# Q, K, V, the gate matrices and the noise laid out by numpy in kernel(), with no transposes of Q and K on the chip

## The chip, the core and the metric

The kernel runs on one core of a Trainium2 chip. The metric is the device time of one execution in microseconds. The core's engines are TensorE (PE, with PEld for its weight loads), VectorE (DVE), ScalarE (ACT), GpSimd (POOL) and SyncE (SP, which here only issues DMAs). What numpy does in `kernel()` before the launch is not part of the metric.

## The reference

Three layers follow each other. Attention comes first: 4 batches, 8 heads, 768 positions, 64 columns per head; each chunk of 32 queries sees 8 memory keys, 16 positions to its left, itself and 8 positions to its right. The result, as 3072 tokens of 512 columns, goes through a soft mixture of 8 experts with 4 slots each, and that through a routed mixture of 8 experts in which every token takes its two best after noise.

```python
k_full = np.concatenate([mem_k, k_ctx], axis=2)      # per chunk of 32 queries
v_full = np.concatenate([mem_v, v_ctx], axis=2)
scores = scale * np.matmul(q_c, k_full.transpose(0, 1, 3, 2))
...                                                  # softmax
out[:, :, c_start:c_end] = np.matmul(a, v_full)
# soft layer: logits = x @ phi; slots = softmax(logits, 0).T @ x; relu(slots @ w1) @ w2; softmax(logits, 1) @ that
# routed layer: logits = x @ w_gate + log1p(exp(x @ w_noise)) * noise; top 2; sum of p * relu(x @ w1) @ w2
```

## The kernel before

**Units and blocks.** Attention runs over 16 units (a batch and a pair of heads), each in two halves of 12 chunks; a half is a block here, 32 in all, `i` in the code. One iteration of the main loop issues for every engine, in a fixed order: the scores of block i+1 (`qk`), their maximum, difference and exponential (`mxr`, `sub`, `expo`), the transpose of the exponentials of block i (`at`, copied by `atc`), the product with V of block i-1 (`av`, divided by `nrm`), and the transpose of the result of block i-2 (`xt`, copied by `xtc`). In every second block the soft layer's logits of a group are multiplied or turned (`lg`, `lt`). Iterations 0 to 27 are this loop; the last four blocks, mixed with the soft layer's first sums, stand in the hand-written list `ORDER`. Each engine takes its instructions strictly in that order.

**Q and K.** `load_raw` brings raw Q or K of a unit as it lies in HBM; `tr` turns it with six fp32 transposes on PE into PSUM, and four copies on ACT put it into `QT` or, with room for the memory keys, into `KB`. `fill_mem` copies the 8 memory keys between the chunks of `KB`, on POOL. `KB` is a block of 128 partitions by two halves: head h lives on partitions 64h to 64h+63 and in half h, and the other half there is zero, so that one matmul computes both heads. There are two `KB`, two `QT` and three raw buffers.

**V.** `load_v` brings V of a block, for each head onto 32 partitions, in rows of 256 B (64 columns of one position). Rows 32 to 55 of a head are the same V one chunk further on, which `shift` copies on the chip (head 0 on DVE, head 1 on POOL); rows 56 to 63 are the memory values, which `mem_rows` copies on POOL. A column of ones gives the sum. There are four such buffers, and `load_v(i + 3)` is issued behind `av(i - 1)`.

**DMA.** All these loads are issued by SP in program order, together with pieces of the soft layer's weights (`load_piece`, 512 KB each, 16 during attention, 48 behind it) and of the output's zeroing (`zero_piece`, by the table `ZA`, 384 KB a step). `KB`, the raw buffers and `VB` lie in a part of `big` that the weights take over when attention is done; so do the outputs `xs` when their sums are done. Behind the 48 pieces SP issues the 8 pieces of the first routed expert (`first_load`). While these flow, the soft layer's experts run on PE; the routed layer starts when its first expert has landed, and takes some 320 us.

**Gates and noise.** Between attention and the soft experts POOL issues five loads: constants, two gate matrices, fp16 constants, and the noise.

Of the kernel before, what the change touches and what calls it, by code (L numbers as in the profile page):

```python
# [14 lines left out]
OP = mybir.AluOpType  # L15
# [15 lines left out]
VC = 130  # L31
# [10 lines left out]
ZA = {2: (0, 1), 13: (1, 2), 17: (2, 3), 21: (3, 4), 25: (4, 5), 26: (5, 7), 27: (7, 8)}  # L42
RA, RB = 26, 44
ORDER = [('qk', 29), ('mx', 29), ('tr', 31), ('sub', 29), ('exp', 29), ('av', 27), ('mv', 29), ('sp', 28), ('nrm', 27), ('lt', 5), ('ltc', 5), ('qk', 30), ('max', 0), ('at', 28), ('atc', 28), ('mx', 30), ('qk', 31), ('col', 0), ('at', 29), ('sub', 30), ('atc', 29), ('pc', 15), ('exp', 30), ('colc', 0), ('av', 28), ('mv', 30), ('sp', 29), ('bc', 0), ('nrm', 28), ('pc', 14), ('xt', 26), ('dsub', 0), ('mx', 31), ('xtc', 26), ('ex', 0), ('sub', 31), ('ldv', 31), ('exp', 31), ('at', 30), ('atc', 30), ('av', 29), ('sp', 30), ('mv', 31), ('sp', 31), ('xt', 28), ('xt', 27), ('mm', 0, 0, 0), ('nrm', 29), ('at', 31), ('atc', 31), ('xtc', 27), ('xtc', 28), ('av', 30), ('nrm', 30), ('xt', 29), ('av', 31), ('xt', 30), ('mm', 0, 0, 1), ('xtc', 29), ('xtc', 30), ('lg', 6), ('nrm', 31), ('mm', 0, 1, 1), ('xt', 31), ('lgc', 6), ('xtc', 31), ('es', 0), ('lg', 7), ('lt', 6), ('lgc', 7), ('lt', 7), ('ltc', 6), ('esp', 0), ('mm', 0, 2, 1), ('ltc', 7), ('mm', 0, 3, 1), ('mm', 0, 1, 0), ('max', 1), ('col', 1), ('mm', 0, 2, 0), ('colc', 1), ('bc', 1), ('dsub', 1), ('fac',), ('mm', 0, 3, 0), ('ex', 1), ('mm', 1, 0, 0), ('facx',), ('out', 0, 0), ('out', 0, 1), ('es', 1), ('mm', 1, 1, 0), ('esp', 1), ('out', 1, 0), ('w',), ('mm', 1, 0, 1), ('mm', 1, 1, 1), ('sit', 0), ('out', 1, 1), ('sitc', 0), ('sit', 1), ('sitc', 1)]
# [82 lines left out]
def tile_kernel(ctx, tc, q, k, v, mem_k, mem_v, phi, sw1, sw2, wg, wn, noise, mw1, mw2, cf_in, c16_in, out):  # L127
# [16 lines left out]
    with ExitStack() as sctx:  # L144
# [28 lines left out]
        with ExitStack() as actx:  # L173
            ab = actx.enter_context(tc.tile_pool(name="ab", bufs=1))
            wk = actx.enter_context(tc.tile_pool(name="wk", bufs=2))
            ps = actx.enter_context(tc.tile_pool(name="ps", bufs=1, space=PSUM))

            attention(tc, nc, q, k, v, mem_k, mem_v, phi, xs, L, K, phis, arena, ab, wk, ps, load_piece, zero_piece)
# [888 lines left out]
def attention(tc, nc, q, k, v, mem_k, mem_v, phi, xs, L, K, phis, arena, ab, wk, ps, load_piece, zero_piece):  # L1067
# [17 lines left out]
    mkT = carve(HP * B * NMEM).rearrange("p (c b m) -> p c b m", c=HP, b=B)  # L1085
    XT = [wk.tile([128, 4, 384], F32, name=f"xT{z}", bufs=1) for z in range(2)]
    mkr = XT[0].rearrange("p j n -> p (j n)")[:H * NMEM, :B * 2 * D].rearrange("p (b z d) -> p b z d", b=B, z=2)
# [6 lines left out]
    QT, ST, A, AT, AV = {}, {}, {}, {}, {}  # L1094

    def load_raw(n):
        u, x = divmod(n, 2)
        b, hp = divmod(u, HP)
        src = (q, k)[x]
        o = src.offset + (b * H + 2 * hp) * S * D  # L1100
        w, r = ((768, 1), (256, 3))[x]
        nc.sync.dma_start(RW[n % 3].rearrange("p (t e) -> p t e", t=r),
                          bass.AP(tensor=src.tensor, offset=o, ap=[[w, 128], [128 * w, r], [1, w]]))

    def vcols(i, p, n, col, cols, c0=0, c1=NH):
        return custom(VB[i % NV][p:p + n], c0 * VC + col, [[VC, c1 - c0], [1, cols]])

    def load_v(i):
        u, z = divmod(i, 2)
        b, hp = divmod(u, HP)  # L1110
        for h in range(2):
            o = v.offset + (b * H + 2 * hp + h) * S * D + NH * z * 32 * D
            c0 = 1 if i == 0 and h == 0 else 0
            c1 = NH if i == 2 * NU - 1 and h == 1 else NH + 1

            def piece(row, n, a, e):
                nc.sync.dma_start(vcols(i, 64 * h + row, n, 66 * h, D, a, e),
                                  bass.AP(tensor=v.tensor, offset=o + (row - 16) * D + a * 32 * D,
                                          ap=[[D, n], [32 * D, e - a], [1, D]]))

            if c0:
                piece(16, 16, 0, 1)
            piece(0, 32, c0, c1)
            if c1 == NH:
                piece(0, 16, NH, NH + 1)

    def mem_rows(i):
        for h in range(2):
            p = 64 * h + 32
            nc.gpsimd.tensor_copy(vcols(i, p, 32, 66 * h, D),  # L1130
                                  mvs[p:p + 32, i // 2:i // 2 + 1, :].to_broadcast([32, NH, D]))
# [5 lines left out]
    def fill_mem(u, eng=nc.gpsimd):  # L1137
        b, hp = divmod(u, HP)
        for h in range(2):
            p = 64 * h  # L1140
            o = custom(KB[u % 2][p:p + 64, h, 32:], 0, [[40, NCH], [1, NMEM]])
            eng.tensor_copy(o, mkT[p:p + 64, hp, b:b + 1, :].to_broadcast([64, NCH, NMEM]))

    def tr(n):
        u, x = divmod(n, 2)
        if x == 0:
            QT[u] = wk.tile([128, S], F32, name="qT")
        p = ps.tile([128, 1024], F32, name="tr", bufs=1)
# [15 lines left out]
        if n + 3 < 2 * NU:  # L1164
            load_raw(n + 3)
# [328 lines left out]
```

## Time and profile before

| | us |
|---|---|
| median of 3 runs (lowest to highest) | 531.72 (531.41 to 531.77) |
| profiled execution, its own time | 533.19 |
| its span in the trace | 531.40 |

The span is what the trace shows between the first and the last instruction; the times of the rows count from its start. A row of the windows gives the stretch, its length, the busy time of PE, PEld, DVE, ACT and POOL with the number of instructions in brackets, the granted clock of PE (1.00 is 2.4 GHz), the busy share of the 16 DMA engines (it can exceed 1, since packets overlap) and the GB/s moved. A row of the timeline or the chain begins with the start and the duration; "x24" is the number of instructions merged in it, and "<-" in brackets names what ended an engine's idle time. In groups by form the two numbers behind the bar are the busy time and the mean duration of one in ns. One qk of a block counts 24 matmuls in the trace, since an fp32 matmul runs as two.

### The profile page before, as it was taken

How to read it: one execution, taken by the hardware profiler on the slowest of the kernel's cores; microseconds unless marked ns; L12 is line 12 of the kernel's file. 1: busy time of each engine (PE TensorE's matmuls, PEld its weight loads, DVE VectorE, ACT ScalarE, POOL GpSimd, SP SyncE). 2: the span in 40 equal slices, each digit the busy share in tenths (PEclk: the TensorE clock that was granted, in tenths of full speed). 3: DMA queues.
4: the chain of work that ended last, by engine and by line, in shares of the span. 5: the costliest groups of instructions: out<-in, count | busy, mean ns of one | idle time of the engine just before them, and what ended most of it. 6: DMA issues, size and time to landing. Idle time of an engine off the chain costs nothing.

```text
span 531.4 us, 12425 instructions
## 1 busy us (share of the span) xinstructions
PE 488.7 (92%) x4854; PEld 271.2 (51%) x4854; DVE 323.9 (61%) x748; ACT 258.7 (49%) x456; POOL 260.2 (49%) x320
## 2 busy tenths in 40 slices
PE   3899998988878888999999999999999999999994
PEld 2666666766433425455454445454544544455441
DVE  6599999989852006896658665674584575552310
ACT  4788887877210206364438254273272462543221
POOL 5877887777030000553735355355336563454223
PEclk9899999999998999999999999999999999999998
DMA  9699999999999999795884939647667773353345
GB/s 201 180 243 237 239 271 241 247 231 316 407 408 358 412 410 344 228 315 169 187 257 107 285 56 222 185 98 189 178 158 166 160 202 48 43 66 44 44 56 64
DMA packets 86178, 109.89 MB, mean 207 GB/s; under 512 B 39408, under 2 KB 52656, under 8 KB 86112
## 3 DMA queue, kind: packets, MB, share of 16 engines
q1 hardware_dynamic: 76240, 93.52, 58.5%
q0 software_dynamic: 9456, 15.36, 20.3%
q8 instruction: 40, 0.66, 0.5%
q14 instruction: 26, 0.21, 0.1%
q10 hardware_dynamic: 416, 0.15, 0.1%
HBM read 88.36 MB, written 20.64 MB: 205 GB/s over the span
## 4 chain that ended last, share of the span: by engine, by line
PE 70%; DMA 14%; ACT 6%; POOL 4%; issue 3%; DVE 2%; POOLq 0%; SPq 0%; DVEq 0%; ACTq 0%
PE l L777 44%; DMA big<-in_v_dram 5%; PE l L747 4%; DMA big<-in_moe_w_dram 3%; PE tr L1153 3%; PE st L1177 3%; PE g L383 2%; ACT big L1163 2%; PE av L1223 2%; PE l L774 2%; PE po L272 2%; DMA w<-in_moe_w_dram 2%; ACT qT L1163 2%; PE p L258 2%; DMA cg<-table,idx 1%
## 5 line engine op out<-in xcount | busy, mean ns | idle before, releaser
L777 PE MATMUL l<-big,hi 128*128 128x512 f16 x768 | 174.2, 379 | 0.2 <-ACT hi L751 0.2
L802 POOL DMA_INDIRECT out_dram<-y,C x46 | 77.5, 1685 | 125.9 <-ACT ctt L709 75.7
L759 DVE SCALAR_TENSOR_TENSOR lo<-l,hi 128x1024 f16<-128x1024 f32 x50 | 61.1, 1222 | 101.5 <-ACT hi L751 101.5
L777 PEld LDWEIGHTS <-hi 128*128 128x128 f16 x768 | 72.6, 98 | 82.7 <-issue 2.9
L796 ACT ACTIVATE y<-l,gw 128x512 f32<-128x512 f32 x44 | 30.1, 685 | 137.6 <-PE l L777 133.6
L777 PE MATMUL l<-big,lo 128*128 128x512 f16 x384 | 90.7, 379 | 0.0
L777 PEld LDWEIGHTS <-lo 128*128 128x128 f16 x384 | 37.4, 98 | 43.6
L1130 POOL COPY big<-big 32x768 f32<-32x768 f32 x64 | 57.1, 893 | 3.7
L635 POOL DMA_INDIRECT cg<-table,C x44 | 46.6, 1059 | 22.0 <-issue 12.2
L751 ACT ACTIVATE hi<-l 128x1024 f16<-128x1024 f32 (+1 forms) x51 | 51.3, 1009 | 6.9 <-PE l L747 2.5
L1163 ACT ACTIVATE qT<-tr 64x384 f32<-64x384 f32 x64 | 33.8, 528 | 17.3 <-PE tr L1153 16.6
L471 DVE SCALAR_TENSOR_TENSOR big<-w,C,big 128x1024 f16<-128x1024 f32 x32 | 40.0, 1278 | 0.2
L1153 PE MATMUL tr<-cf,big 128*128 128x128 f32 x192 | 30.9, 300 | 8.4 <-DMA cf<-in_const_f_dram 4.7
L467 ACT ACTIVATE big<-w,C 128x1024 f16<-128x1024 f32 x32 | 35.6, 1149 | 3.1 <-DVE C L422 2.9
L1135 POOL COPY big<-big 24x768 f32<-24x768 f32 x32 | 27.1, 848 | 18.9 <-DMA big<-in_v_dram 17.6
L1177 PE MATMUL st<-big,qT 128*32 128x128 f32 (+2 forms) x768 | 29.6, 286 | 6.0 <-ACT big L1163 2.8
L1163 ACT ACTIVATE big<-tr 64x384 f32<-64x384 f32 x64 | 33.0, 515 | 4.1 <-PE tr L1153 3.2
L1223 PE MATMUL av<-big,aT 128*32 128x130 f32 x768 | 28.1, 279 | 3.8 <-PE at L1208 1.6
L1153 PEld LDWEIGHTS tr<-cf,big 128*128 128x128 f32 x192 | 22.5, 150 | 15.2 <-issue 5.6
L747 PE MATMUL l<-ctt,big 128*128 128x128 f16 x384 | 29.3, 219 | 0.0
L395 DVE TENSOR_REDUCE mxp<-w 128x1 f32<-128x2048 f32 x12 | 27.3, 2277 | 0.0
L1177 PEld LDWEIGHTS st<-big,qT 128*32 128x32 f32 x768 | 20.6, 114 | 12.5 <-ACT big L1163 6.0
(274 smaller groups left out, 640.1 us busy)
## 6 DMA issues: line engine op xcount, KB each, us to landing
w<-in_moe_w_dram SPq DMA_DIRECT2D x72, 512.0 KB, 7.2
big<-in_moe_w_dram SPq DMA_DIRECT2D x56, 512.0 KB, 10.0
big<-in_v_dram SPq DMA_DIRECT2D x62, 104.0 KB, 6.1
big<-in_q_dram SPq DMA_DIRECT2D x16, 384.0 KB, 6.0
big<-in_k_dram SPq DMA_DIRECT2D x16, 384.0 KB, 6.6
out_dram<-zt SPq DMA_DIRECT2D x2, 1536.0 KB, 12.4
out_dram<-zt SPq DMA_DIRECT2D x6, 384.0 KB, 5.8
out_dram<-zt SPq DMA_DIRECT2D x1, 768.0 KB, 5.3
```

What stands on the lines that cost most here:

```text
L471: stt(lo, w2, sc[:, rk, 5:6], hi, op0=OP.mult, op1=OP.subtract)
L635: b = nc.gpsimd.indirect_dma_start(out=CG[i][:, 32:], out_offset=None, in_=table, in_offset=bass.IndirectOffsetOnAxis(ap=icol(c), axis=0))
L747: nc.tensor.matmul(p[:, k, :], GT[i][:, 128 * k:128 * k + 128], CTT[i], start=True, stop=True)
L751: nc.scalar.activation(HI[i][:, k], p[:, k], AF.Relu)
L759: stt(LO[i].rearrange("p k t -> p (k t)"), p.rearrange("p k t -> p (k t)"), 0.0, HI[i].rearrange("p k t -> p (k t)"), op0=OP.max, op1=OP.s ...
L777: nc.tensor.matmul(P2[i], h[i][:, k, :], dyn(W2f, i, w * 4096 + 512 * k, 512, RG.get(i)), start=x == 0 and k == 0, stop=x == last and k == 7)
L802: b = nc.gpsimd.indirect_dma_start(out=out, out_offset=bass.IndirectOffsetOnAxis(ap=icol(c), axis=0), in_=y, in_offset=None, compute_op=OP ...
L1130: nc.gpsimd.tensor_copy(vcols(i, p, 32, 66 * h, D), mvs[p:p + 32, i // 2:i // 2 + 1, :].to_broadcast([32, NH, D]))
L1153: nc.tensor.transpose(p[:, y, 128 * t:128 * t + 128], RW[n % 3][:, 128 * i:128 * i + 128], identf)
L1163: nc.scalar.activation(o, i, AF.Copy)
L1177: nc.tensor.matmul(st[32 * j:32 * j + 32, g, :, w0:w1], QT[u][:, 32 * c:32 * c + 32], kb[:, :, 40 * c + w0:40 * c + w1], start=True, stop= ...
L1223: nc.tensor.matmul(p[32 * j:32 * j + 32, g, :], AT[i][:, g, 32 * j:32 * j + 32], VB[i % NV][:, c:c + 130], start=True, stop=True, tile_pos ...
```

## The change

`arranged` in `kernel()` prepares the inputs with numpy. Q is transposed for each unit (128 rows of 768 columns). K is transposed and laid out just as a half of `KB` holds it, with the memory keys in place: 984 columns for each of 128 rows. V is laid out for each block and head as 32 rows of 13 chunks of 65 columns, the column of ones included. The gate matrices are joined and, like the noise, stored by partition.

On the chip `load_raw`, `tr`, `fill_mem`, the mem_k loads and their transposes go. `load_k` brings K with two loads of 64 partitions straight into `KB`, `load_q` brings Q with one; both have three buffers now, and unit u+3 is loaded behind the scores of unit u. `load_v` writes one row of 3,380 B per partition; a V buffer now holds its two heads one behind the other. In the loop the shift of head 0 and the copy `xtc` are on ACT; in `ORDER` they stay on DVE. Two V buffers are cleared inside iterations 0 and 1, eight matmuls on zeros stand at the start, and `ZA` spreads the same eight steps of zeros differently. `ORDER` loses its one `tr`.

```diff
-VC = 130
+VC = 65
...
-ZA = {2: (0, 1), 13: (1, 2), 17: (2, 3), 21: (3, 4), 25: (4, 5), 26: (5, 7), 27: (7, 8)}
+ZA = {5: (0, 1), 9: (1, 2), 13: (2, 3), 17: (3, 4), 21: (4, 5), 25: (5, 6), 26: (6, 7), 27: (7, 8)}
...
-        nc.gpsimd.dma_start(wgn[:, :, 0:8], wg.rearrange("(j p) e -> p j e", p=128))
-        nc.gpsimd.dma_start(wgn[:, :, 8:16], wn.rearrange("(j p) e -> p j e", p=128))
+        nc.gpsimd.dma_start(wgn.rearrange("p j e -> p (j e)"), wgn_in)
...
-        nc.gpsimd.dma_start(nz, noise.rearrange("(t p) e -> p t e", p=128))
+        nc.gpsimd.dma_start(nz.rearrange("p t e -> p (t e)"), noise)
...
-    KB = [carve(2 * KB_W).rearrange("p (h w) -> p h w", h=2) for i in range(2)]
-    RW = [carve(2 * S * D // 128) for i in range(3)]
-    VB = [carve((NH + 1) * VC) for i in range(NV)]
+    KB = [carve(2 * KB_W).rearrange("p (h w) -> p h w", h=2) for i in range(3)]
+    QT = [carve(S) for i in range(3)]
+    HB = (NH + 1) * VC
+    VB = [carve(2 * HB) for i in range(NV)]
...
+    def load_k(u):
+        for h in range(2):
+            p = slice(64 * h, 64 * h + 64)
+            nc.sync.dma_start(KB[u % 3][p, h, :], k[u][p])
+
+    def load_q(u):
+        nc.sync.dma_start(QT[u % 3], q[u])
+
+    def vcols(i, p, n, h, cols, c0=0, c1=NH, o=0):
+        return custom(VB[i % NV][p:p + n], h * HB + c0 * VC + o, [[VC, c1 - c0], [1, cols]])
...
+            nc.sync.dma_start(VB[i % NV][64 * h:64 * h + 32, h * HB:h * HB + HB], v[i, h])
...
-    def shift(i):
-        for h, eng in ((0, nc.vector), (1, nc.gpsimd)):
-            eng.tensor_copy(vcols(i, 64 * h + 32, 24, 66 * h, D), vcols(i, 64 * h, 24, 66 * h, D, 1, NH + 1))
...
+    def shift(i, fast=None):
+        nc.gpsimd.tensor_copy(vcols(i, 96, 24, 1, D), vcols(i, 64, 24, 1, D, 1, NH + 1))
+        o, x = vcols(i, 32, 24, 0, D), vcols(i, 0, 24, 0, D, 1, NH + 1)
+        if fast:
+            nc.scalar.activation(o, x, AF.Copy)
+        else:
+            nc.vector.tensor_copy(o, x)
...
-                c = (4 * g + j) * VC
+                c = custom(VB[i % NV], (4 * g + j) * VC, [[HB, 2], [1, VC]])
...
+        if fast:
+            nc.scalar.activation(XT[z][:, hp, :], p, AF.Copy)
+        else:
+            nc.vector.tensor_copy(XT[z][:, hp, :], p)
...
+    load_k(0)
+    load_q(0)
+    load_v(0)
+    load_k(1)
+    load_q(1)
+    load_v(1)
+    load_v(2)
+    load_k(2)
+    load_q(2)
+    load_v(3)
+    for h in range(2):
+        nc.gpsimd.memset(KB[0][64 * h:64 * h + 64, 1 - h], 0.0)
...
+    pw = ps.tile([128, 3, 130], F32, name="pw", tag="av", bufs=1)
+    for x in range(8):
+        nc.tensor.matmul(pw[:, 0, 0:128], zt[:, 0:128], zt[:, 128:256], start=True, stop=True)
...
+    clear(0, nc.vector)
+    clear(1, nc.vector)
+    for u in range(1, 3):
+        for h in range(2):
+            nc.gpsimd.memset(KB[u][64 * h:64 * h + 64, 1 - h], 0.0)
...
-        tr(i + 3)
-        if s == 1:
-            fill_mem(u + 2)
         if i == 6:
             nc.gpsimd.dma_start(phis, phi.rearrange("(j p) s -> p j s", p=128))
         sub(n)
         expo(n)
-        shift(i)
+        if i < 2:
+            clear(i + 2, nc.vector)
+        shift(i, True)
+        if i == 0:
+            mem_rows(2)
         at(i)
         atc(i)
+        if s == 0 and u + 3 < NU:
+            load_k(u + 3)
+            load_q(u + 3)
...
-            xtc(i - 2)
+            xtc(i - 2, True)
...
+def arranged(x):
...
+    x["q"] = x["q"].reshape(units, 2, S, D).transpose(0, 1, 3, 2).reshape(units, 128, S)
+    kt = x["k"].reshape(units, 2, S, D).transpose(0, 1, 3, 2).reshape(units, 128, NCH, 2, 16)
+    mk = x["mem_k"].reshape(units, 2, NMEM, D).transpose(0, 1, 3, 2).reshape(units, 128, 1, NMEM)
+    kb = np.zeros((units, 128, KB_W), np.float32)
...
+    vb = np.ones((units, 2, 2, 32, nh + 1, VC), np.float32)
...
+    x["v"] = vb.reshape(2 * units, 2, 32, (nh + 1) * VC)
...
     arrays, args = {}, []
+    inputs = arranged(inputs)
```

## Rows read from the trace of the kernel before

**Rows 1.** The page, part 1: busy us (share of the span) x instructions.
```profile
PE 488.7 (92%) x4854; PEld 271.2 (51%) x4854; DVE 323.9 (61%) x748; ACT 258.7 (49%) x456; POOL 260.2 (49%) x320
```

**Rows 2.** Windows: busy us of each engine, granted clock, DMA share, GB/s.
```profile
40.00:60.00 20.00, 18.53 (x340) 13.80 (x343) 18.28 (x48) 16.67 (x33) 16.49 (x23) 1.00 1.13 237
60.00:80.00 20.00, 18.54 (x320) 13.12 (x310) 18.19 (x48) 16.58 (x34) 17.04 (x23) 1.00 1.15 260
...
140.00:150.00 10.00, 9.26 (x108) 4.26 (x104) 7.07 (x18) 1.82 (x5) 0.00 (x0) 1.00 1.04 412
```

**Rows 3.** Timeline of SP's DMA issues after attention (us, duration).
```profile
128.46 60.25 SPq L161 DMA_DIRECT2D big<-in_moe_w_dram  x48
189.50 9.22 SPq L216 DMA_DIRECT2D w<-in_moe_w_dram  x8
```

**Rows 4.** The chain that ended last, behind the soft stage (us, duration).
```profile
193.31 10.23 DMA w<-in_moe_w_dram
```

**Rows 5.** Timeline: scores of blocks 0 and 1, 2, 29 and 31.
```profile
13.51 2.78 PE L1177 MATMUL st<-big,qT 128*32 128x96 f32 x48
...
19.30 1.20 PE L1177 MATMUL st<-big,qT 128*32 128x96 f32 x24 [1.69 <-POOL big L1142]
...
124.22 0.86 PE L1177 MATMUL st<-big,qT 128*32 128x128 f32 x24
...
129.34 0.86 PE L1177 MATMUL st<-big,qT 128*32 128x128 f32 x24
```

**Rows 6.** The chain that ended last, inside attention.
```profile
38.06 7.94 DMA big<-in_v_dram
...
86.37 0.80 PE tr L1153 x6
```

**Rows 7.** Groups by form to 170 us: busy us, mean ns | idle before.
```profile
L1163 ACT ACTIVATE qT<-tr 64x384 f32<-64x384 f32 x64 | 33.8, 528 | 17.3 <-PE tr L1153 16.6
...
L1135 DVE COPY big<-big 24x768 f32<-24x768 f32 x32 | 24.6, 771 | 1.0
...
L1253 DVE COPY xT<-xt 128x384 f32<-128x384 f32 x32 | 17.4, 548 | 1.2 <-PE xt L1246 1.2
...
L1214 ACT ACTIVATE aT<-at 128x384 f32<-128x384 f32 x32 | 15.7, 491 | 3.4 <-PE at L1208 2.7
...
L1142 POOL COPY big<-big 64x192 f32<-64x192 f32 x30 | 10.7, 358 | 8.5 <-PE st L1177 3.8 <-DVE big L1412 3.3
...
L190 POOL DMA_DIRECT2D nz<-in_moe_noise_dram x1 | 1.4, 1427 | 0.0
...
L250 ACT ACTIVATE C<-C 128x768 f32<-128x768 f32 x1 | 0.8, 842 | 5.4 <-DVE C L249 5.4
...
L187 POOL DMA_DIRECT2D wgn<-in_moe_w_gate_dram x1 | 0.8, 752 | 0.0
...
L184 POOL DMA_DIRECT2D cfb<-in_const_f_dram x1 | 0.6, 568 | 18.9 <-DVE phis L1376 18.9
```

**Rows 8.** Windows: V's loads nearly alone; Q's and a weight piece's.
```profile
16.60:18.20 1.60, 1.00 (x8) 0.57 (x6) 1.51 (x4) 1.44 (x4) 1.48 (x3) 1.00 1.17 192
18.90:20.80 1.90, 1.50 (x26) 1.15 (x27) 0.23 (x3) 1.31 (x3) 1.78 (x4) 0.70 0.97 381
```

**Rows 9.** DMA issues to 170 us: count, KB each, median us to landing.
```profile
big<-in_v_dram SPq DMA_DIRECT2D x62, 104.0 KB, 6.1
big<-in_q_dram SPq DMA_DIRECT2D x16, 384.0 KB, 6.0
big<-in_k_dram SPq DMA_DIRECT2D x16, 384.0 KB, 6.6
w<-in_moe_w_dram SPq DMA_DIRECT2D x8, 512.0 KB, 7.2
out_dram<-zt SPq DMA_DIRECT2D x6, 384.0 KB, 5.8
```

More of the change, by code (lines that the diff above doesn't have):

```diff
@@ L126, in tile_kernel @@
 @with_exitstack
-def tile_kernel(ctx, tc, q, k, v, mem_k, mem_v, phi, sw1, sw2, wg, wn, noise, mw1, mw2, cf_in, c16_in, out):
+def tile_kernel(ctx, tc, q, k, v, mem_v, phi, sw1, sw2, wgn_in, noise, mw1, mw2, cf_in, c16_in, out):
     nc = tc.nc
@@ L176, in tile_kernel @@
             ps = actx.enter_context(tc.tile_pool(name="ps", bufs=1, space=PSUM))
-            attention(tc, nc, q, k, v, mem_k, mem_v, phi, xs, L, K, phis, arena, ab, wk, ps, load_piece, zero_piece)
+            attention(tc, nc, q, k, v, mem_v, phi, xs, L, K, phis, zt, arena, ab, wk, ps, load_piece, zero_piece)
         mid = ctx.enter_context(tc.tile_pool(name="mid", bufs=1, side="right"))
@@ L1064, in experts, with attention @@
                 put(i)
-def attention(tc, nc, q, k, v, mem_k, mem_v, phi, xs, L, K, phis, arena, ab, wk, ps, load_piece, zero_piece):
+def attention(tc, nc, q, k, v, mem_v, phi, xs, L, K, phis, zt, arena, ab, wk, ps, load_piece, zero_piece):
     scale = D ** -0.5
@@ L1170, in qk @@
         st = ps.tile([128, 3, 2, 64], F32, name="st", bufs=2)
-        kb = KB[u % 2]
+        kb = KB[u % 3]
         for g in range(3):
@@ L1231, in nrm @@
         rc = wk.tile([128, 3, 2], F32, name="rc")
-        nc.vector.tensor_scalar(rc, p[:, :, D:D + 2], 1.0e-9, None, op0=OP.add)
+        nc.vector.tensor_scalar(rc, custom(p, D, [[130, 3], [65, 2]]), 1.0e-9, None, op0=OP.add)
         nc.vector.reciprocal(rc, rc)
@@ L1247, in xt, with xtc @@
         XP[i] = p
-    def xtc(i):
+    def xtc(i, fast=None):
         u, z = divmod(i, 2)
@@ L1376, in d_sitc @@
         nc.vector.tensor_copy(phis[:, 2 * h:2 * h + 2], M[0, h])
-    load_raw(0)
-    load_raw(1)
-    for z in range(2):
-        (nc.scalar, nc.gpsimd)[z].dma_start(mkr[:, :, z, :], mem_k.rearrange("b h m d -> (h m) b d"))
+    load_k(0)
[10 more added lines that the diff above has]
+        nc.gpsimd.memset(KB[0][64 * h:64 * h + 64, 1 - h], 0.0)
     for h in range(2):
@@ L1468, in attention @@
         ops[o[0]](*o[1:])
-_INS = ["q", "k", "v", "mem_k", "mem_v", "moe_phi", "moe_w1", "moe_w2", "moe2_w_gate", "moe2_w_noise", "moe2_noise",
-        "moe2_w1", "moe2_w2"]
+_INS = ["q", "k", "v", "mem_v", "moe_phi", "moe_w1", "moe_w2", "gates", "moe2_noise", "moe2_w1", "moe2_w2"]
+def arranged(x):
+    import numpy as np
+    x = {n: np.asarray(a) for n, a in x.items()}
+    units, nh = B * HP, NCH // 2
+    x["q"] = x["q"].reshape(units, 2, S, D).transpose(0, 1, 3, 2).reshape(units, 128, S)
+    kt = x["k"].reshape(units, 2, S, D).transpose(0, 1, 3, 2).reshape(units, 128, NCH, 2, 16)
+    mk = x["mem_k"].reshape(units, 2, NMEM, D).transpose(0, 1, 3, 2).reshape(units, 128, 1, NMEM)
+    kb = np.zeros((units, 128, KB_W), np.float32)
+    cols = kb[:, :, :40 * NCH].reshape(units, 128, NCH, 40)
+    cols[..., 16:32] = kt[..., 0, :]
+    cols[..., 32:40] = mk
+    for c in range(NCH):
+        kb[:, :, 40 * c + 40:40 * c + 56] = kt[:, :, c, 1]
+    x["k"] = kb
+    vp = np.zeros((units, 2, S + 32, D), np.float32)
+    vp[:, :, 16:16 + S] = x["v"].reshape(units, 2, S, D)
+    vb = np.ones((units, 2, 2, 32, nh + 1, VC), np.float32)
+    for z in range(2):
+        w = vp[:, :, 32 * nh * z:32 * nh * z + 32 * (nh + 1)].reshape(units, 2, nh + 1, 32, D)
+        vb[:, z, :, :, :, :D] = w.transpose(0, 1, 3, 2, 4)
+    x["v"] = vb.reshape(2 * units, 2, 32, (nh + 1) * VC)
+    g = np.concatenate([x["moe2_w_gate"], x["moe2_w_noise"]], axis=1)
+    x["gates"] = g.reshape(4, 128, 2 * E).transpose(1, 0, 2).reshape(128, 8 * E)
+    x["moe2_noise"] = x["moe2_noise"].reshape(NT, 128, E).transpose(1, 0, 2).reshape(128, NT * E)
+    return x
 def kernel(**inputs):
```

103 lines of the change are left out of this document (12 added, 91 removed).

## Prediction

> **What bounds the kernel now.** I read the page first, then the stages, the chain, the groups of instructions, the DMA rates. The page says that PE is busy for nine tenths of the span [rows 1], but that is a mean over three stages. In the attention stage (to about 130 us) PE, DVE, ACT and POOL are all 82 to 93% busy and the DMA engines count as full too, at 237 to 260 GB/s; from about 135 us on the other engines thin out, and the DMA stays full at 412 GB/s [rows 2]. So there are two questions: who sets the pace of attention, and does time won there reach the end?
>
> The second first. After attention SP issues 48 pieces of soft weights and 8 of the first expert in one unbroken stretch, and the chain that ends last goes through the landing of exactly these, to 203.54 us [rows 3, 4]. These 56 pieces are 29.4 MB (56 x 512 KB); at 412 GB/s they take 71.3 us, so they must have begun to flow without a break at 203.5 - 71.3 = 132.2 us. That moment, call it the hand-over, is when attention's own transfers are through. The expert stage behind it is not touched. Whatever moves the hand-over moves the end by as much.
>
> Now the pace of attention. Block 2's scores start at 19.30 and block 29's at 124.22: 27 blocks in 104.9 us, 3.89 us each [rows 5]. With the busy shares of the stretch from 40 to 60 us that makes, for each block, 3.60 us on PE (93%), 3.55 on DVE, 3.24 on ACT and 3.2 on POOL [rows 2]. The chain in this stage changes hands between PE, ACT's copies of transposed Q and K and, from 38 us on, loads of V that POOL's shift waits for [rows 6]. No engine alone is the bound: a block is the longest engine's work plus some 8% of handing over (3.89 against 3.60).
>
> The DMA's share has to be read with care, because a share over 1 only says that packets overlap. Priced by stretches in which one kind of load is nearly alone: V, in rows of 256 B onto 32 partitions, flows at 192 GB/s; raw Q and weights, in rows of 3 and 4 KB onto 128 partitions, at 381 [rows 8]; the weights' stretch at 412 [rows 2]. I take 350 for raw K (rows of 1 KB, but onto all 128 partitions: between the two, nearer to the second) and 400 for Q and the zeros. With the sizes of [rows 9]: V 6.8 MB / 192 = 35.5 us, K 6.29 / 350 = 18.0, Q 6.29 / 400 = 15.7, zeros 3.15 / 400 = 7.9, sixteen weight pieces 8.39 / 412 = 20.4; together 97.5 us of the 130.7 between 1.5 (about when the first transfers flow) and the hand-over. So the DMA has about 33 us of slack before the change, and the engines set the pace.
>
> **The change, part by part.** *Transposes of Q and K.* PE loses six fp32 transposes a block, 0.80 us [rows 6]; ACT loses four copies at 0.53, 2.1 us. In the loop ACT takes over two things: the half of the shift that was DVE's (0.77 there; on ACT I price it by the only 768-wide row of ACT, 0.84) and the copy out of xt (0.55 on DVE; 0.49 by ACT's copy of the same shape). POOL loses the fills of mem_k, two of 0.36 every other block [rows 7]. A block becomes 2.8 us on PE, 3.24 - 2.1 + 0.84 + 0.49 = 2.47 on ACT, 3.55 - 0.77 - 0.55 = 2.23 on DVE and 2.85 on POOL. Bounds for the shift on ACT: 0.49 (the 384-wide copy) to 1.7 (twice the 768-wide row); even then ACT stays under 3.4, which the range holds.
>
> *The start.* Before, block 0's scores wait for tr(0), the mem_k transposes, tr(1) and eight copies, and begin at 13.51 [rows 5]. After, they wait for the landing of K0 and Q0 alone. The first two loads before take 3.7 and 5.2 us to land [rows 9]; K0 is two DMAs and Q0 a third, so I put block 0 at 6.5 and, with the clears of two V buffers on DVE ahead of its max, block 2 at about 10. This is 9 us of engine time, gained only if the DMA keeps up.
>
> *The transfers.* This is where the gain can be lost. K arrives with mem_k and gaps laid out: 984 columns a row, 504 KB a unit against 384, so 8.06 MB against 6.29, and no longer as one load onto 128 partitions but as two loads of 64 partitions with rows of 3,936 B. V brings its column of ones: 211 KB a block against 208, 6.92 MB, still two loads onto 32 partitions each, but in rows of 3,380 B instead of 256. Q keeps its size, in rows of 3,072 B. The trace shows no load onto fewer than 128 partitions with long rows. Its price lies between V's 192 GB/s (same partitions, short rows) and 412 (long rows, all partitions) [rows 2, 8]. I take 210: the nearest row is the one with the same partitions, with a tenth added for the rows that are thirteen times longer. Then K 8.06 / 210 = 38.4 us and V 6.92 / 210 = 33.0; Q, zeros and weights stay at 44.0 (the zeros are only spread over other blocks); sum 115.4 us. At 412 it is 19.6 + 16.8 + 44.0 = 80.4 us, at 192 it is 122.0.
>
> Against the engines: a block at 2.85 us plus the same 8% is 3.1, and since the load of V now stands in ACT's own order ahead of the copy of A, I take 3.2. 27 x 3.2 = 86 us from block 2 at 10 gives block 29 at 96. The DMA at 210 needs 115.4 + 1.5 = 117 and so becomes the bound; a queue that is always fed still loses something at the start and around the last loads of V, for which I add 2.5. Hand-over at 119.4 instead of 132.2: 12.8 us earlier.
>
> The Trainium skill has a rule for this, on its page "SBUF — State Buffer", section "Door 1": a transfer onto 64 partitions reaches only half of the ports of the memory, at best 218 GB/s, and the section "Can I just issue two DMAs to hit both halves?" says that a pair of such transfers does not overlap. By the row the sum is 115.4; by that page's 218 it would be 37.0 + 31.7 + 44.0 = 112.7 (an estimate). The row of V agrees with it in size, but cannot tell it from short rows.
>
> *Gates and noise.* Two POOL loads of 0.75 and one of 1.43 us become two of about 0.55 (as cfb, the same 128 rows each): some 1.8 us less on POOL at 154 to 158 us [rows 7]. PE's first accumulation of the soft stage waits for it, but the weights' stream runs on underneath and ends last [rows 3, 4]: counted at nothing; without that cover it would be 1.8. *PSUM, the tail and the V layout:* the tail loses one block of transposes and the strides in av and nrm change; same sizes, counted at nothing, covered by the same stream. Their bounds: -1 to +1 us.
>
> Sum: -12.8 us on the profiled span of 531.40. The median of the runs shown is 531.72, 0.3 above that span (the profiled execution itself took 533.19): 519.
>
> **The rivals.** *Long rows move at full speed.* If V's 192 GB/s comes from its 256 B packets and not from its partitions, the DMA needs 80 us and the engines set the pace: block 29 at 96. Before, the hand-over came 8.0 us behind block 29, with V still queued; block 31's scores, which the first of the 56 pieces waits for, came 5.1 behind it [rows 5]. I take 6.5: hand-over at 102.5, 29.7 us earlier: 502. For it: V's stretch counts a DMA share of 1.17 at 192 GB/s, the weights' 1.04 at 412 [rows 2, 8], so its short packets take long. Against: all that it moved went onto 32 partitions. On its page "DMA: Bandwidth & Descriptors", section "Why small descriptors are slow", the Trainium skill names such a cost per packet; if it were the whole of it, the result would be this rival's.
>
> *The half loads are the bound and the loop doesn't keep the queue fed.* V is issued only when a buffer comes free after av, and now its lateness holds up ACT, so exp and the copy of A behind it, so the next av and the next issue. If K and V get 175 GB/s, a tenth less than V's row, 46.1 + 39.5 + 44.0 = 129.6 us, and a quarter of the 33 us of slack before stays as holes (8), the hand-over is at 139: 7 us later, 539. It decides once K and V together fall below about 187 GB/s with such holes (1.5 + 44 + 8 + 14.98 MB / rate = 133.3). For it: V's landing already stands in the chain from 38 us on [rows 6]. Against: with three units of K and Q and four of V in buffers, some 2 MB can be outstanding.
>
> *Neither, rates between.* At 250 GB/s the DMA needs 103.9, hand-over 108, 507; this belongs to the forecast's own spread.
>
> **How the numbers follow.** Forecast (DMA-bound, half loads at 192 to 250) 0.57: 507 to 528, the upper end being 192 GB/s with 5 us of holes. Full speed 0.27: 497 to 507. Slower by holes 0.10. The remaining 0.06 is for what I have not seen, spread evenly over both sides. The range that holds 8 in 10 is 499 to 528: it takes in most of the first rival, and leaves out the tail above and the fastest corner. About 0.2% (1 us) is what a measurement of this kernel can tell from no change. Faster 0.87, within it 0.04, slower 0.09.
>
> **What would show it.** In the changed profile: no copies out of tr on ACT, PE at some 70% in attention. If the forecast holds, the chain in attention is mostly loads of V and K, at about 290 GB/s with the DMA full, and a stretch with only K and V in flight shows about 210. If the first rival holds, such a stretch shows 350 or more, PE or ACT fill the chain, and a block takes 3.2 us. In all cases the 56 weight pieces still take 71 us and end last before the experts. I am wrong in kind if the hand-over moves and the end doesn't move with it, or if the loop is slower than both the DMA's sum and 3.2 us a block.

## The result, and the profile after

| | before | after |
|---|---|---|
| median of 20 runs, us | 531.33 (529.07 to 533.50) | 526.88 (523.77 to 532.63) |
| ratio, 95% interval | | 0.9909 [0.9891, 0.9927] |
| profiled execution: own time, span, us | 533.19, 531.4 | 526.26, 524.5 |

The ratio is that of the means and leaves out one slow execution of the changed kernel, the 532.63.

Faster by 4.5 us by the medians, 3.9 to 5.8 by the interval. The forecast was 519, or 12.8 us faster: right in direction, too large by more than a factor of two. The time lies inside both ranges that were given.

The page of the changed kernel, part 1, and two of its DMA issues up to 170 us (count, KB each, median us to landing):

```profile
PE 469.1 (89%) x4674; PEld 253.3 (48%) x4674; DVE 288.7 (55%) x689; ACT 224.8 (43%) x382; POOL 242.4 (46%) x290
...
big<-in_k_dram SPq DMA_DIRECT2D x32, 246.0 KB, 7.3
big<-in_v_dram SPq DMA_DIRECT2D x64, 105.6 KB, 6.3
```

PE lost 20 us of work, DVE 35 and ACT 34 [rows 1]; the end came 7 us earlier in this pair of profiles. So most of the engine time that was saved did not shorten the kernel. The windows of after that answer to [rows 2]:

```profile
40.00:60.00 20.00, 15.81 (x316) 10.75 (x316) 12.66 (x40) 11.29 (x22) 12.05 (x15) 1.00 1.05 270
60.00:80.00 20.00, 16.66 (x312) 11.66 (x316) 11.84 (x38) 13.11 (x24) 14.42 (x18) 0.91 1.05 276
140.00:150.00 10.00, 7.35 (x92) 3.77 (x96) 6.41 (x18) 2.33 (x6) 2.72 (x6) 1.00 1.04 413
```

All four engines have come off their 82 to 93%, PE to about 80% and the others to 56 to 72%, and only the DMA share still stands above 1. The chain between 28 and 110 us says what they wait for: 77.6% of it are landings of V (35.4% before), one behind the other. Five of its longest pieces (start, us):

```profile
28.94 7.72 DMA big<-in_v_dram
...
37.20 7.59 DMA big<-in_v_dram
...
44.87 0.59 ACT big L1119
45.46 6.99 DMA big<-in_v_dram
...
53.24 6.73 DMA big<-in_v_dram
```

SP's own waits between 20 and 115 us tell the same. Before, SP held its next load back for an engine, PE above all; after, it waits for its earlier transfers to land: 42.3 of 50.2 us of its waits, against 1.1 of 55.9. The two longest, first of before, then of after (us in total, times, longest):

```profile
SPq L1117 <- PE av L1223: 18.9, 21, 1.4
SPq L1102 <- PE tr L1153: 12.7, 11, 3.9
```
```profile
SPq L1097 <- DMA big<-in_k_dram: 9.7, 16, 0.8
SPq L161 <- DMA w<-in_moe_w_dram: 5.8, 4, 1.7
```

The groups by form, for the copies that were priced, and the scores of blocks 0 and 1, 2 and 29 in the timeline, against [rows 7] and [rows 5]:

```profile
L1119 ACT ACTIVATE big<-big 24x768 f32<-24x768 f32 x28 | 23.6, 844 | 13.4 <-DMA big<-in_v_dram 13.0
...
L1211 ACT ACTIVATE xT<-xt 128x384 f32<-128x384 f32 x26 | 12.7, 490 | 0.5 <-PE xt L1202 0.5
```
```profile
7.25 2.34 PE L1133 MATMUL st<-big 128*32 128x96 f32 x48 [2.52 <-DMA big<-in_q_dram]
12.77 1.51 PE L1133 MATMUL st<-big 128*32 128x96 f32 x24 [1.52 <-POOL big L1112]
...
112.75 0.86 PE L1133 MATMUL st<-big 128*32 128x128 f32 x24
```

The shift on ACT takes 844 ns (842 was priced), and the xt copy 490. From block 2 to block 29 a block takes 3.70 us, against 3.89 before and 3.2 by the engines in the forecast. SP's issues behind attention, against [rows 3]:

```profile
119.12 58.60 SPq L161 DMA_DIRECT2D big<-in_moe_w_dram  x48
178.60 9.17 SPq L215 DMA_DIRECT2D w<-in_moe_w_dram  x8
```

The weights start 9.3 us earlier in this pair and the first expert is issued 10.9 earlier, but the span ends only 6.9 earlier. The difference lies at the very end, where POOL runs a drain and then the last three scatters. POOL's timeline there, first of before, then of after (start, us, [idle before, what ended it]):

```profile
512.79 1.55 POOL L802 DMA_INDIRECT out_dram<-y,C  x1 [4.00 <-DMA out_dram<-y,C]
519.07 0.09 POOL L800 MEMSET spacer<- 1x1 f32 x1 [4.72 <-issue]
519.81 1.55 POOL L802 DMA_INDIRECT out_dram<-y,C  x1 [0.66 <-ACT y L796]
...
524.57 1.55 POOL L802 DMA_INDIRECT out_dram<-y,C  x1 [1.31 <-ACT y L796]
```
```profile
502.60 1.55 POOL L801 DMA_INDIRECT out_dram<-y,C  x1 [3.76 <-DMA out_dram<-y,C]
511.87 0.09 POOL L799 MEMSET spacer<- 1x1 f32 x1 [7.72 <-issue]
512.92 1.55 POOL L801 DMA_INDIRECT out_dram<-y,C  x1 [0.96 <-issue]
...
516.64 1.55 POOL L801 DMA_INDIRECT out_dram<-y,C  x1 [0.27 <-issue]
```

Between the scatter and the spacer's memset stands the drain. POOL is idle there for 4.72 us before and 7.72 after. Before, the first and the last of the three scatters behind it still wait for their tiles ("<-ACT y"); after, the tiles are there and the scatters queue up behind the drain ("<-issue"). These two waits, "the drain wait" below, are what the experiments follow at the end; at the front they follow SP's 48 pieces, their start and their duration.

### The profile page after: what moved, and what is told of

It reads as the page before. It is cut to its first block, busy times and chain, and to the rows that moved or that the text cites. A ratio compares the mean times of both kernels' runs of the same rounds, so it can differ in the third digit from the quotient of the medians.

```text
span 524.5 us, 11862 instructions
## 1 busy us (share of the span) xinstructions
PE 469.1 (89%) x4674; PEld 253.3 (48%) x4674; DVE 288.7 (55%) x689; ACT 224.8 (43%) x382; POOL 242.4 (46%) x290
## 4 chain that ended last, share of the span: by engine, by line
PE 62%; DMA 23%; DVE 4%; issue 4%; ACT 3%; POOL 2%; POOLq 1%; SPq 0%; ACTq 0%; DVEq 0%
PE l L776 43%; DMA big<-in_v_dram 12%; DMA big<-in_moe_w_dram 5%; PE l L746 4%; PE g L382 3%; PE l L773 2%; DMA w<-in_moe_w_dram 2%; DMA out_dram<-y,C 2%; PE av L1179 1%; DMA big<-in_q_dram 1%; PE st L1133 1%; PE po L271 1%; ACT big L1119 1%; PE p L257 1%; POOL big L1368 1%
## 5 line engine op out<-in xcount | busy, mean ns | idle before, releaser
L801 POOL DMA_INDIRECT out_dram<-y,C x46 | 76.6, 1664 | 126.5 <-ACT ctt L708 82.9
L1112 POOL COPY big<-big 32x768 f32<-32x768 f32 x64 | 53.1, 830 | 4.3 <-DMA big<-in_mem_v_dram 0.7
L1164 PE MATMUL at<-cf,a 128*128 128x128 f32 x96 | 18.4, 303 | 19.9 <-ACT aT L1170 17.5
L1133 PE MATMUL st<-big 128*32 128x128 f32 (+2 forms) x768 | 30.6, 298 | 4.0 <-DMA big<-in_q_dram 2.5
L1179 PE MATMUL av<-big,aT 128*32 128x130 f32 x768 | 30.5, 293 | 3.5 <-DMA big<-in_moe_w_dram 2.5
L1159 ACT ACTIVATE a<-a 128x384 f32<-128x384 f32 x32 | 16.8, 525 | 35.4 <-DVE a L1154 26.9
L1119 ACT ACTIVATE big<-big 24x768 f32<-24x768 f32 x28 | 23.6, 844 | 13.4 <-DMA big<-in_v_dram 13.0
L746 PEld LDWEIGHTS <-big 128*128 128x128 f16 x384 | 23.7, 98 | 6.2 <-issue 0.2
L1133 PEld LDWEIGHTS st<-big 128*32 128x32 f32 x768 | 21.8, 119 | 9.7 <-issue 3.7
```

What stands on the lines that cost most here:

```text
L746: nc.tensor.matmul(p[:, k, :], GT[i][:, 128 * k:128 * k + 128], CTT[i], start=True, stop=True)
L801: b = nc.gpsimd.indirect_dma_start(out=out, out_offset=bass.IndirectOffsetOnAxis(ap=icol(c), axis=0), in_=y, in_offset=None, compute_op=OP ...
L1112: nc.gpsimd.tensor_copy(vcols(i, p, 32, h, D), mvs[p:p + 32, i // 2:i // 2 + 1, :].to_broadcast([32, NH, D]))
L1133: nc.tensor.matmul(st[32 * j:32 * j + 32, g, :, w0:w1], QT[u % 3][:, 32 * c:32 * c + 32], kb[:, :, 40 * c + w0:40 * c + w1], start=True, s ...
L1179: nc.tensor.matmul(p[32 * j:32 * j + 32, g, :], AT[i][:, g, 32 * j:32 * j + 32], c, start=True, stop=True, tile_position=(0, 32 * j))
```

## The experiments

**The same two kernels again.** No edit.

> The kernel before, once more, for a second profile. Theory 1 (the end of an execution varies by itself: POOL's drain ahead of the last three scatters takes more or less time, whatever came earlier): the stretch from the last scatter before the drain to the next instruction on POOL, 6.3 us in the first profile (512.79 to 519.07), differs by 1 us or more, and the start of the second expert's 32 gate matmuls stays at 232.3 within 1 us. Theory 2 (the drain is longer only in the changed kernel): 6.3 within 0.5 us again.

> The changed kernel, once more, with times. Theory 1: the gate matmuls of the second expert start at 221.7 within 1.5 us again (10.6 earlier than before), the stretch around the drain, 9.3 us in the first profile, differs by 1 us or more, and the ratio is near 0.99. Theory 2: 9.3 within 0.5 us again, and the time is 4 to 5 us below before.

before_2: 531.62 us once, drain wait 4.81. after_2: 525.95 us, ratio 0.9912 [0.9883, 0.9942], drain wait 7.43. SP's rows of before_2 and after_2:

```profile
125.35 59.95 SPq L161 DMA_DIRECT2D big<-in_moe_w_dram  x48
```
```profile
122.19 58.31 SPq L161 DMA_DIRECT2D big<-in_moe_w_dram  x48
```

The start of the pieces differs by 3 us between executions of one kernel, so the 9.3 us of the first pair are no measurement. The drain wait is steady, as theory 2 has it.

**K onto 128 partitions.** The same bytes as one transfer, into one half of the buffer, so the score matmuls mix the two heads.

```
-        for h in range(2):
-            p = slice(64 * h, 64 * h + 64)
-            nc.sync.dma_start(KB[u % 3][p, h, :], k[u][p])
+        nc.sync.dma_start(KB[u % 3][:, 0, :], k[u])
...
```

> K of a unit comes with one load onto all 128 partitions, the same bytes, into one half of the buffer; both heads then share a half, so the scores aren't the reference's. Theory A (a load onto 64 partitions runs at about 200 GB/s, one onto 128 at 400, and the DMA's sum sets the pace): K's 16 units cost 20 us and not 38 to 40, so the gate matmuls of the second expert start 15 to 19 us earlier than 221.7, at 203 to 207, unless the engines then set the pace at 3.2 us a block, which gives 205. Theory B (the DMA moves mixed traffic at some 275 GB/s whatever the partitions, or the engines are the bound): 220 to 222.

513.52 us, ratio 0.967 [0.9641, 0.97]. The second expert's gate matmuls start at 210.80, between theory A's 203 to 207 and theory B's 220 to 222. SP's row, and two windows with a faster flow and busier engines than after's:

```profile
108.02 58.86 SPq L161 DMA_DIRECT2D big<-in_moe_w_dram  x48
```
```profile
40.00:60.00 20.00, 17.82 (x362) 12.29 (x364) 13.77 (x44) 14.21 (x26) 14.06 (x18) 1.00 1.03 301
60.00:80.00 20.00, 17.82 (x366) 12.22 (x354) 13.77 (x44) 14.43 (x27) 14.55 (x18) 1.00 1.04 304
```

Rows and bytes of K are the same; one transfer onto 128 partitions stands in place of two onto 64. So the half-width landing of K costs about 13 us in the whole kernel. That the number of transfers has a part in it was not tried separately; against it, the DMA share is over 1 with either, so no gaps between transfers show. The mixed heads don't explain the gain: from the second expert's gate matmuls to the end it is 302.0 us, as in after_2 (301.9). What bounds k_one is not shown: PE is at 89%, and the DMA share still at 1.03.

**No zeros.** The output's rows stay unzeroed.

```
             load_v(i + 3)
-            zero_piece(i)
```

> The changed kernel without the eight pieces that write zeros to out_dram in attention (3 MB; the output's rows are not zeroed). If the transfers set attention's pace, the hand-over comes earlier by about what the pieces take of the engines, 3.1 MB at 390 GB/s = 8 us, so the second expert's gate matmuls start 6 to 8 us earlier (about 214 to 217 in the profile, against 221.7 and 225.1) and the time is 519 to 521. If the engines set the pace, nothing moves: 526 to 527.

521.08 us, ratio 0.9799 [0.9766, 0.9833]; gate matmuls at 218.56, just short of what was expected. SP's row:

```profile
116.19 58.64 SPq L161 DMA_DIRECT2D big<-in_moe_w_dram  x48
```

Transfers do set attention's pace. Of the 8 us that the zeros were estimated at, 5.8 come back in the medians and 4.4 in the start of the pieces (116.2 in one execution against 120.6, the mean below). Whether the rest is a queue that is not always fed, or zeros that cost less than estimated, is not shown; SP's waits between 20 and 115 us are still mostly for landings (41.0 of 50.0 us).

**The two copies back on DVE.**

```
-        shift(i, True)
+        shift(i)
-            xtc(i - 2, True)
+            xtc(i - 2)
```

> The changed kernel with the shift of head 0's V rows and the xT copies of the block loop back on DVE. If the transfers set attention's pace, DVE's added 1.3 us in a block fit in (2.3 us of 3.6 now) or cost a little: 526 to 530. If the gain came from taking them off DVE, the time goes back to 531 or more.

528.35 us, ratio 0.9955 [0.9930, 0.9979], pieces at 125.48 in an execution of 530.02, with DVE at 18.2 of 20 us. Inside the first expectation: 1.5 us slower than after by the medians. Moving the copies to ACT is worth a part of the gain: with DVE this busy, SP's waits for PE grow from 2.9 to 11.7 us, while those for landings still lead with 30.4.

**No drain in the loop.**

```
-        if n == len(seq) - 4:
-            nc.gpsimd.drain()
```

> The changed kernel without the explicit drain of POOL near the end. Theory 1: if the wait for the drain is what the end pays for, the last scatter follows the last y by 0.3 us as in the kernel before, and the time falls by 2 to 4 us against the changed kernel (ratio to before 0.983 to 0.987). Theory 2' (the drain is only moved: the conditional part behind the loop drains POOL anyway): no change within 1 us, or slower by up to 2 us.

530.93 us, ratio 0.9994 [0.9971, 1.0017]: 4 to 5 us slower than after, more than either theory allowed. The last scatter is issued in time (515.83), but the span ends at 529.3: the wait has only moved behind the last scatter, where nothing covers it.

**More POOL instructions; more POOL transfers.**

```
+        if 10 <= i < 25:
+            for x in range(2):
+                nc.gpsimd.memset(one, 1.0)
```

> The changed kernel with 30 one-column memsets of the tile `one` on POOL added in attention (two in each of blocks 10 to 24; 290 POOL instructions become 320, as many as before). Theory: the changed kernel waits 7.4 to 7.7 us after POOL's drain, against 4.7 to 4.8 before, because POOL's next instructions have to be fetched there (in its trace two packets of the instruction queues follow the landing of the scatter one after the other, before only one lies under it), and where the fetches fall depends on how many instructions stand ahead. Then the idle time ahead of the spacer's memset after the drain returns to 4.5 to 5.2 us and the time falls by 2 to 3 us, to 523 to 525. Rival: the wait belongs to the scatters or to what the change did to the queues; then it stays at 7.4 to 7.7 us and the time stays at 526 to 527.

525.47 us, ratio 0.9906 [0.9879, 0.9933], drain wait 7.46: with as many POOL instructions as before the wait is unchanged, so the theory of instruction fetches, as it was put, fell.

```
-        nc.gpsimd.dma_start(wgn..., wgn_in)
+        for x in range(2):
+            nc.gpsimd.dma_start(wgn...[:, 32 * x:32 * x + 32], wgn_in[:, 32 * x:32 * x + 32])
...
```

> The changed kernel with the gate matrices and the noise each loaded in two halves, so that POOL issues as many DMAs as before (two more). If the wait after the drain hangs on how many DMAs POOL has issued before (which of its lanes the last scatters use), it returns to 4.5 to 5.2 us; by the theory of instruction fetches two instructions are too few to move it, and it stays at 7.4 to 7.7 us.

528.45 us once, drain wait 8.02: two more transfers don't shorten it either.

**POOL's old transfers back, all and in parts.** pool_dma loads gates and noise in their old shapes and POOL's half of mem_k into a buffer that nothing reads; mem_k_only and gates_only do one of the two.

```
-        nc.gpsimd.dma_start(wgn.rearrange("p j e -> p (j e)"), wgn_in)
+        nc.gpsimd.dma_start(wgn[:, :, 0:8], wg.rearrange("(j p) e -> p j e", p=128))
+        nc.gpsimd.dma_start(wgn[:, :, 8:16], wn.rearrange("(j p) e -> p j e", p=128))
...
-        nc.gpsimd.dma_start(nz.rearrange("p t e -> p (t e)"), noise)
+        nc.gpsimd.dma_start(nz, noise.rearrange("(t p) e -> p t e", p=128))
```

> The changed kernel with POOL's DMAs as before: gate matrices and noise loaded in their old shapes, and POOL's half of mem_k loaded into a buffer that nothing reads. If the longer drain comes from the state of POOL's DMA queue (which entries of it the last scatters use, 9376 packets in the changed kernel against 9456), the drain takes 6.4 us again in place of 9.1 to 9.5 and the time falls by 2 to 3 us, to 523 to 525. Rival: it comes from elsewhere; then the drain stays at 9.1 to 9.5 us, and since the gate and noise loads were counted at nothing, the time stays at 526 to 528.

> The changed kernel with POOL's old load of mem_k alone (64 KB in rows of 256 B, into a buffer that nothing reads). With all of POOL's old loads back the drain took 6.5 us. If the mem_k load is what sets the state of POOL's queue, the drain is 6.4 to 6.6 us here and 9.1 to 9.5 us with the gate and noise loads alone. If it is the sum of what POOL's queue has carried, both of the two stay at 9.1 to 9.5 or only one changes. Time: 524 to 526 with the short drain, 526 to 528 with the long one.

> The changed kernel with the gate matrices and the noise alone loaded as before (two loads in pieces of 32 B for the gates, one of the noise). The counterpart of the run with mem_k alone: the drain 9.1 to 9.5 us if mem_k's load decides, 6.4 to 6.6 us if these three do. By the prediction's step, which counted this edit at nothing, the second expert's gate matmuls start no later than in the changed kernel (221 to 225).

The spacer's row of pool_dma, of mem_k_only and of gates_only:

```profile
511.55 0.09 POOL L800 MEMSET spacer<- 1x1 f32 x1 [5.05 <-issue]
```
```profile
511.72 0.09 POOL L799 MEMSET spacer<- 1x1 f32 x1 [7.57 <-issue]
```
```profile
510.39 0.09 POOL L800 MEMSET spacer<- 1x1 f32 x1 [4.40 <-issue]
```

So the loads of the gates and the noise set the drain wait, mem_k's doesn't. But the times did not fall as expected: 525.72, ratio 0.9909 [0.9881, 0.9936], 525.58, 0.9902 [0.9869, 0.9935], and 525.09, 0.9895 [0.9857, 0.9933]. SP's rows of pool_dma and gates_only tell why:

```profile
120.32 60.22 SPq L161 DMA_DIRECT2D big<-in_moe_w_dram  x48
```
```profile
119.60 60.81 SPq L161 DMA_DIRECT2D big<-in_moe_w_dram  x48
```

With the old loads the 48 pieces take 60 us or more again. What the drain wins, the weights' stretch loses.

**That edit alone, on the kernel before.** The new gate and noise loads, all else as before.

> The kernel before with the new loads of the gate matrices and the noise alone. In all runs with the new loads SP's 48 weight pieces after attention are issued in 56.5 to 58.9 us, in all with the old ones in 60.0 to 60.8; and POOL's spacer memset after the drain waits 7.4 to 8.0 us with the new ones, 4.4 to 5.1 with the old ones (without a second drain). If this edit makes two effects that cancel, the 48 pieces take 57 to 59 us here, the wait is 7.4 us or more, and the time stays within 1.5 us of the kernel before. If the wait hangs on something else of the change, it is 4.7 us here and the time falls by about 2 us.

531.15 us, ratio 1.0007 [0.9985, 1.0029], as expected. SP's row and POOL's:

```profile
125.83 57.42 SPq L161 DMA_DIRECT2D big<-in_moe_w_dram  x48
```
```profile
516.54 0.09 POOL L799 MEMSET spacer<- 1x1 f32 x1 [7.37 <-issue]
```

Both effects are there and cancel.

**Where the drain stands.** The drain two tiles earlier (drain_early), or a second one eight tiles earlier (two_drains).

```
-        if n == len(seq) - 4:
+        if n == len(seq) - 6:
```
```
-        if n == len(seq) - 4:
+        if n in (len(seq) - 12, len(seq) - 4):
```

> The changed kernel with the drain two tiles earlier. There the scatters are not yet the last work, so a wait of 9.4 us is made up: the scatters behind it catch up before the last tile, the last scatter is issued within 1 us of the last tile's y, and the time falls by 2.5 to 3.5 us, to 523 to 524.5, if that wait is what the changed kernel loses at the end. If it is not, 526 to 528.

> The changed kernel with a second drain on POOL eight tiles earlier. In the run without the explicit drain, the drain at the very end took 6.0 us with no transfer in flight, while in the other runs the last drain, which follows one by 17 us, took 0.29 us. If a drain's time is work saved up since the drain before it, the one at the old place shrinks, to 4.7 us or less (the landing of the scatter alone), the last scatter is issued within 1 us of the last tile, and the time falls by 2.5 to 4 us, to 522.5 to 524.5. If it is fixed, the late drain stays at 9.1 to 9.5 us and the time stays at 526 to 528, or more for the stop at the earlier drain.

523.98 us, ratio 0.9860 [0.9834, 0.9885], and 523.08, 0.9864 [0.9836, 0.9891]: both as expected and, by the ratios, some 2.5 us better than after, with intervals that just clear or touch its [0.9891, 0.9927]. With a drain before it, the late one is short, and the last scatter waits for its tile again; in drain_early the scatters have caught up by then. two_drains:

```profile
507.55 0.09 POOL L799 MEMSET spacer<- 1x1 f32 x1 [3.94 <-issue]
...
513.88 1.55 POOL L801 DMA_INDIRECT out_dram<-y,C  x1 [1.84 <-ACT y L795]
```

**A version that beats both.** K dense on 128 partitions, the score matmuls split by head (64 rows, 64 columns), the heads in two PSUM banks. k_dense has one score buffer, k_dense2 two and the second drain, k_dense3 also a fifth V buffer.

```
-                nc.tensor.matmul(st[32 * j:32 * j + 32, g, :, w0:w1], QT[u % 3][:, 32 * c:32 * c + 32],
-                                 kb[:, :, 40 * c + w0:40 * c + w1], ..., tile_position=(0, 32 * j))
+                for h in range(2):
+                    p = slice(64 * h, 64 * h + 64)
+                    nc.tensor.matmul(st[32 * j:32 * j + 32, h, g, w0:w1], QT[u % 3][p, 32 * c:32 * c + 32],
+                                     kb[p, 40 * c + w0:40 * c + w1], ..., tile_position=(64 * h, 32 * j))
```

> The changed kernel with K in one 128-partition transfer of the same bytes and the score matmuls split by head: 24 matmuls over 64 rows and 64 columns in place of 12 over 128 and 128, the two heads in two banks, without the zero blocks and their memsets, and the subtraction in four instructions in place of two. It computes the reference. If half-partition transfers are what costs, it comes near the run with K in one transfer (513.5), plus what the split matmuls add: with 0.2 to 0.5 us more on PE and 0.3 us more on DVE in each of 32 blocks, 512 to 522. If K's transfers were no limit it is 527 or more.

> K in one 128-partition transfer with score matmuls by head, as before, but the scores in two buffers of two banks in place of one, and a second drain eight tiles earlier. It computes the reference. Theory: the first form lost its gain because a block's scores had to be read before the next block's could be written (its transfers ran at 0.81 to 0.95 of the engines, so they no longer set the pace). Then the second expert's gate matmuls start at 211 to 217 (210.8 in the run with K in one transfer and the old matmuls) and, with 299.6 us from there to the end, the time is 512 to 519. Rival: the doubled number of PE instructions is what costs; then they start at 220 or later and the time is 522 to 524, the two drains alone.

> As k_dense2, with a fifth buffer for V, so that a block's V is issued one block earlier. In the changed kernel the chain from 28 to 110 us is for 78% landings of V of some 7 us each, one behind the other, since a buffer has to come free before the next load is issued. If it is this circle that sets the pace, one buffer more takes 2 us or more from k_dense2's 518.5. If it is the rate of the transfers alone, nothing changes: 517.5 to 519.5.

k_dense: 525.40, ratio 0.9887 [0.9849, 0.9925], no better than after by more than the intervals tell, and above what was expected if K's landing is what costs; pieces at 121.40, DMA share 0.81 to 0.95, so its transfers did not set the pace. k_dense2: **518.46, ratio 0.9766 [0.9732, 0.9801]**; some 2.5 us of the gain are the second drain's, by the run above. SP's row:

```profile
114.91 57.99 SPq L161 DMA_DIRECT2D big<-in_moe_w_dram  x48
```

Two score buffers thus bring the pieces forward by 6.5 us. Landings of V are 10.4% of its chain from 28 to 110 us, against 77.6% after, and SP waits for engines again (3.2 of 50.3 us for landings). k_dense3: 522.74, 0.9870 [0.9828, 0.9912], slower than k_dense2, which neither expectation had. Block 31's scores start at 114.23, in k_dense2 at 114.15, so in this pair of profiles V's four buffers were not the limit left. Behind them the weight pieces stall. The window from 120 to 130 us, of k_dense2 and of k_dense3:

```profile
120.00:130.00 10.00, 8.12 (x120) 5.12 (x119) 8.11 (x24) 2.02 (x4) 0.82 (x1) 0.89 1.04 408
```
```profile
120.00:130.00 10.00, 8.44 (x122) 5.38 (x121) 8.11 (x24) 2.02 (x4) 0.00 (x0) 0.87 0.66 229
```

In k_dense3 a piece waits for a shift of V on DVE, as SP's waits from 100 to 180 us show:

```profile
SPq L161 <- DVE big L1119: 5.0, 1, 5.0
```

All V buffers lie where soft weights are to land. By the code, block 31's V stands in the second of five buffers there and in the last of four in k_dense2, and the pieces reach the second sooner. That this is the whole of the loss was not tried.

## Why the prediction was wrong

**What held.** Direction; the engines come off the bound, the transfers of K and V become it; the chain is mostly landings of V; the shift on ACT as priced (844 ns for 842); block 0 at 7.25 (6.5 forecast); the 48 pieces follow right behind the last loads of V. The first rival (long rows move at full speed) is refuted for K: its rows are 3,936 B in after and in k_one, where one transfer onto 128 partitions replaces two onto 64. For V, on 32 partitions, it wasn't tried.

The Trainium skill, page "SBUF — State Buffer", section "Door 1", says that a transfer onto 64 partitions reaches half of the ports. k_one agrees: between 40 and 80 us it flows at 301 to 304 GB/s against after's 270 to 276, and the pieces start 12.6 us earlier (108.0 against 120.6). That ports are the reason, no run here shows.

**The step that failed: the transfers, "hand-over at 119.4 instead of 132.2: 12.8 us earlier".** The mechanism was right, the size off. Ten executions with after's attention stage (after, after_2, after_nodrain, pad_i, pad_d, pool_dma, mem_k_only, gates_only, drain_early, two_drains) start the 48 pieces at 119.1 to 123.0, mean 120.6; three with before's (before, before_2, before_gates) at 125.4 to 128.5, mean 126.5. So attention got 5.9 us shorter, not 12.8.

The same executions show where. Block 2's scores start 6.6 us earlier (12.7 against 19.3 on the mean), and from there to block 29 a block takes 3.73 us against 3.80. Nearly all that was won is the start without transposes; in the loop the transfers hold the pace about where the engines held it before.

Of the 6.9 missing, 1.9 lie in the execution that the forecast was made against: at 128.46 [rows 3] its pieces were the latest of the three and its own time was 533.19, but the 12.8 was taken off the median of 531.72. The other 5.0 (120.6 against 128.46 - 12.8 = 115.7) are transfers. With Q, zeros and weights as priced and the 2.5 us for holes as added, K and V took 71.4 + 5.0 = 76.4 us instead of 71.4, so by these prices 196 GB/s where 210 was taken: the tenth that was added to V's 192 for longer rows did not come. SP's waits for landings, and the flow of 279 GB/s between 20 and 100 us (269 in after_2) at a DMA share of 1.04, where about 290 was forecast, point to rate more than to holes. How the 5.0 divides exactly stays open, since no stretch has K and V alone in flight. Block 2 at 12.77 instead of 10, behind POOL's copy of the memory rows, is a smaller miss of the start.

**"Gates and noise ... counted at nothing" was right by cancelling.** Under the weights' stream this edit was not free: the 48 pieces take 56.5 to 58.9 us with the new loads (14 executions, k_dense3 aside, mean 58.0) and 60.0 to 60.8 with the old (4, mean 60.3), so it saves 2.3 us; the cover that was named, the stream itself, is what the small loads slowed.

**"The expert stage behind it is not touched" failed.** It looked at the work of the expert stage and not at POOL's queue at its end, which the gate and noise loads do touch. With one late drain and the new gate and noise loads, the drain wait is 7.4 to 8.0 us, with the old ones 4.4 to 5.1. From the second expert's gate matmuls to the span's end it is 302.0 us in ten executions with the long wait (301.4 to 303.2), and 299.3 in four with the old loads (299.0 to 299.6): 2.7 us lost. "Whatever moves the hand-over moves the end by as much" held as far as it was tried: in k_one, with the same long wait, the pieces start 12.6 us earlier than in after and the time is 13.4 us less.

Together: -5.9 - 2.3 + 2.7 = -5.5, so 5.5 us faster, against 4.5 (3.9 to 5.8) measured.

Of the second rival (half loads the bound, and the loop starves the queue) one half came: the rate fell short of 210, to 196, and stayed above the 187 that this rival needed. The starved queue did not show in SP's waits.

## What to carry to other kernels

Ask of a layout not only whether its rows are long but onto how many partitions one transfer lands: K in halves left attention 12.6 us behind K whole, more than twice the 5.9 that the change won there, and a dense K with matmuls by head gets about half of it back (114.9 against 120.6). A sum against one profile inherits that execution's luck, here 1.9 us of a stage; profile twice before pricing a few per cent. Follow a gain to the last instruction: a drain or a queue just before the end can hold it back, and a drain set earlier, while there is still work to cover it, costs less.

## What the runs showed of the hardware

A drain on POOL was not only a wait for transfers in flight. In after it lasted from 502.4 to 511.8, but the last packet of POOL's queue was through at 507.1, 4.8 us before POOL went on. This empty part was 4.8 to 5.2 us in the ten runs with one late drain and the new gate and noise loads, 1.8 to 2.1 in the four with the old ones, and 1.0 in two_drains and k_dense2, behind an earlier drain. So all of the difference lies behind the transfers. With the drain taken out of the loop, some 12 us lay between the last scatter's end (517.4) and the span's end (529.3), where it is 6.3 in after. How long the drain waits depended on the shape of three small loads of 32-byte pieces made some 350 us earlier, and not on the 30 instructions or the two transfers added. Why, no run shows.

Those loads, 128 KB in all, slowed 25 MB of weights in another queue by 2.3 us.
